# Order of SyncE's transfers in a fused top-k attention and MLP kernel: outputs and values ahead of the transposing transfers, queries and keys half a pair sooner

## The chip, the cores and the metric

The kernel runs on one core of one Trainium2 chip. A core has TensorE (PE; its weight loads are shown apart as PEld), VectorE (DVE), ScalarE (ACT), GpSimd (POOL) and SyncE (SP). SyncE computes nothing: it issues the transfers of this kernel, one after the other in program order, and sixteen DMA engines carry them out. The metric is the device time of one execution in microseconds (us).

## The reference

Two blocks follow each other. The first is attention over 8 batches of 8 heads, 576 positions and head size 64, in which every query keeps its 32 largest scores:

```python
scores = scale * np.matmul(q, k.transpose(0, 1, 3, 2))
kth = np.partition(scores, -top_k, axis=-1)[..., -top_k:-top_k + 1]
scores = np.where(scores >= kth, scores, -1000000000.0)
attn = np.exp(scores - max); attn = attn / (sum + 1e-09)
attn_out = np.matmul(attn, v)
```

The second takes the attention output as 4608 rows of 512 and sends them through a hidden layer of 2048: `h = x @ w_in`, `g = h * sigmoid(1.702 * h)`, `out = g @ w_out`. Everything is float32.

## The kernel before, in words

**Slots and pairs.** The work of the attention is cut into 144 slots, 18 for each batch `b`. A slot is 128 query rows of two heads: of one pair of heads `hp` (16 full slots of a batch, `t` = 0 to 3 and `hp` = 0 to 3), or the last 64 rows of two pairs of heads (two "ends" slots). An even batch has its full slots first and then its ends, an odd batch the other way round. From slot 25 on (`COLLECTED`), the function `joined_pair(n)` does one pair of slots `n`, `n + 1` per call, so `n` is odd, and what engines do within a pair is in the order in which this function calls things. Everything before is in an order written out by hand (`ORDER`), which the change does not touch.

**What happens to one slot.** TensorE computes the scores into PSUM, ScalarE copies them out (`sc`), VectorE finds the 32 largest by rounds of MAX8 and MATCH_REPLACE8 on `ranked`, ScalarE masks and takes exponentials (`pr`), GpSimd divides by the sum (`normalize`). Then the probabilities have to be transposed. `split` (line 613) lets ScalarE separate the 16-bit halves and writes them to DRAM (`rows`), and `turn_by_dma` (line 621) reads them back with a transposing transfer into `pt`. `pt` has two buffers, so a new transposing transfer can only be issued once TensorE has read the buffer of two slots before. From `pt` and the values `v_l`, `v_e`, TensorE computes the attention output.

**TensorE's run of scores.** Once per pair, `joined_section` (line 1426) runs on TensorE: first the attention outputs of slots `n - 5` and `n - 4` (matmuls into the tile `mixed`, reading `pt` and `v_l`), then the scores of two new slots (`s_ps`). It reads the values of slot `n - 5` first and, after 32 matmuls, those of slot `n - 4`. In the pairs that begin at the slots `18 b + 1` and `18 b + 3` these are the last slots that use the values of batch `b - 1`; the list `VALUES` (line 972) therefore makes `load_v` due there: heads in two halves at `18 b + 1` and `18 b + 3` for an even `b`, both halves at `18 b + 3` for an odd `b`.

**The MLP beside it.** `hidden` puts the first layer into the tile `unit`, `project` the second into the two banks `po`, in four units for each block of 128 rows, two units per pair; so a block is complete every second pair. Then `leave_parts` (line 921) lets ScalarE bring the banks to `raws`, GpSimd adds the parts up in two portions of three operations (`merge_some(3)`), and the last of them puts the output's two DMAs (`bring_out`, line 936) on a list `writes`. `write_all` (line 426) issues what is on that list. The next `leave_parts` writes the same part of `raws`, and so has to wait until these DMAs have read it.

**Queries and keys.** For each pair of heads, `load_both` (line 390) issues four DMAs into the one buffer `qk_l`; two or more slots later `prepare_by_dma` (line 394) lets ScalarE split them into `halves`, which frees the buffer; these are written to DRAM (`qk_rows`), and a transposing transfer brings them into `qk_t` later still. When these fall due stands in `READY` (line 969); `dues` (line 1207) collects what is due in the two slots of a pair, and `begin(0)` and `begin(1)` issue it in the middle and at the end of the pair.

**SyncE's order within a pair**, before: the transposing transfer of slot `n - 3` (`turn_due`); `rows` of slot `n - 1`; the transposing transfer of `n - 2`; `write_all` (outputs and `qk_rows`); `begin(0)` (values, queries and keys); `rows` of slot `n`; `write_all`; `begin(1)`.

Of the kernel before, what the change touches and what calls it, by code (L numbers as in the profile page):

```python
# [145 lines left out]
def kernel(  # L146
# [279 lines left out]
    def write_all():  # L426
        while writes:
            writes.pop(0)()
# [27 lines left out]
    PER = N // B  # L456
    st = [{} for _ in slots]

    def head_at(n, i):

        return 1 - i if n % 2 and slots[n][0] > 0 else i
# [76 lines left out]
    def exponentials(n, between=lambda: None):  # L538

        mask(n)  # L540
        between()
        exps(n)
# [78 lines left out]
    def turn_by_dma(n):  # L621

        rows = st[n]["rows"]
        pt = st[n]["pt"] = ptp.tile([P, 2 * NF + 1, P], F32, name="pt")
        nc.sync.dma_start_transpose(out=pt[:].bitcast(U16), in_=rows[:].rearrange("q h k -> (q h) k"))
# [330 lines left out]
    def leave_all():  # L956
        while leaving:
            leaving.pop(0)()
# [4 lines left out]
    def at(n, fn, *args):  # L963
        later.setdefault(n, []).append((fn, args))
# [4 lines left out]
    READY = (-15, -11, -7, -3), (-17, -13, -9, -5)  # L969
# [16 lines left out]
    for b in range(1, B):  # L986
        for hp in range(NP):
            if b > 1:
                earlier = 2 * ((b, hp) > (2, 1))
                at(b * PER + (READY[b % 2][hp] - 4 if earlier else (-19, -13)[hp]), load_both, b, hp)  # L990
                if (b, hp) != (2, 0):
                    at(b * PER + READY[b % 2][hp] - earlier, prepare_by_dma, b, hp)
            else:
                at(b * PER + FETCH_1[hp], load_both, b, hp)
        for hps, n in VALUES[b % 2 if b == 1 else b % 2 + 2].items():
            at(b * PER + n, load_v, b, *hps)
# [210 lines left out]
    def dues(n):  # L1207

        preparing = (prepare_by_dma,)
        todo = [later.pop(m, []) for m in (n, n + 1)]  # L1210
        assert not any(fn in preparing for fn, _ in todo[1])

        def begin(i):
            for fn, args in todo[i]:
                if fn not in preparing:
                    fn(*args)

        some = [(fn, args) for fn, args in todo[0] if fn in preparing]

        def prepare_some():  # L1220
            if some:
                fn, args = some.pop(0)
                fn(*args)

        return begin, prepare_some
# [3 lines left out]
    def find(m, at):  # L1229

        for i, op in enumerate(topk(m) if live(m) else [lambda: None] * 14):
            op()
            if i == 7 and live(m) and live(m + 1):
                pair_up(m + 1)
            if i == at and live(m - 1):
                invert(m - 1)
            if i > 1 and len(unfinished) > (2 if m == SETTLED + 1 else 0):
                finish_one()
# [187 lines left out]
    def joined_section(new, held):  # L1426

        begun = set()
        ends, rest = [], []
        for s, m in enumerate(held):  # L1430
            b, t, hps = slots[m]
            pt = st[m]["pt"]
            for p in range(2 if t == NF else 1):
                cols = slice(p * TAIL, (p + 1) * TAIL) if t == NF else slice(0, P)
                to = slice(s * P + cols.start, s * P + cols.stop)
                main, tail = vv[b, hps[p]]
                for i in range(2):
                    on, j = slice(i * TAIL, (i + 1) * TAIL), head_at(m, i)
                    ends.append((i, j, to, tail[on, j, :], pt[on, NF, cols]))
                for c in range(NF):  # L1440
                    for i in range(2):
                        rest.append((None, head_at(m, i), to, main[:, head_at(m, i), c, :], pt[:, MAIN[i] + c, cols]))
            st[m].clear()

        def score(n, i, p, first, count):
            b, t, hps = slots[n]
            cols = slice(t * P + p * TAIL, t * P + (p + 1) * TAIL) if t < NF else slice(FULL, S)
            on = slice(head_at(n, i) * D, (head_at(n, i) + 1) * D)
            keys = slice(FIRST[i] + first, FIRST[i] + first + count)
            return qT[b, hps[p]][on, cols], kT[b, hps[p]][on, keys]  # L1450

        def last_keys(r):
            of = [(n, head_at(n, r), p) for n in new for p in range(2)]
            at = lambda n, i: TAILS + n % 2 * P + i * TAIL
            return [(r, p, slice(at(n, i), at(n, i) + TAIL), *score(n, i, p, FULL, TAIL)) for n, i, p in of]

        def first_keys(n, r):
            i = head_at(n, r)
            for p in range(2):
                to = score_banks[n % 2][p * TAIL : (p + 1) * TAIL, i, :]  # L1460
                lhsT, rhs = score(n, i, p, 0, FULL)
                nc.tensor.matmul(to, lhsT=lhsT, rhs=rhs)

        upper = [x for x in ends if x[0] == 0] + last_keys(0)
        lower = last_keys(1) + [x for x in ends if x[0] == 1]
        halves = [x[1] for x in rest + upper + lower]
        count = iter(range(len(halves)))

        def mix(parts):
            for _, j, cols, lhsT, rhs in parts:  # L1470
                k = next(count)
                nc.tensor.matmul(
                    joined[0][j * D : (j + 1) * D, cols],
                    lhsT=lhsT,
                    rhs=rhs,
                    start=j not in halves[:k],
                    stop=j not in halves[k + 1 :],
                )

        def mark():  # L1480
            nc.tensor.drain(fusable=True).then_inc(parted, 1)
            parts_done.append(None)

        mix(rest)
        ahead = max(0, min(2, len(upper) - 2))
        mix(upper[:ahead])
        for n in new[:1]:
            first_keys(n, 1)
        mix(upper[ahead:-1])
        mark()  # L1490
        mix(upper[-1:])
        mark()
        for n in new[:1]:
            first_keys(n, 0)
        for n in new[1:]:
            first_keys(n, 1)
            first_keys(n, 0)
        nc.tensor.wait_ge(parted, len(parts_done))
        mix(lower)

    def copy_keys(n):
        sc = st[n]["sc"] = keys_ring[0].tile([P, 2, S], F32)
        nc.scalar.copy(out=sc[:, :, 0:FULL], in_=main_keys(n))

    def copy_last_keys(n):
        nc.scalar.copy(out=st[n]["sc"][:, :, FULL:S], in_=tails(n))

    def project_next():
        leave_all()
        project_one()  # L1510

    def turn_due(m):
        if live(m) and m > COLLECTED - 2:
            turn_by_dma(m)

    def joined_pair(n):

        begin, prepare_some = dues(n)
        held = [m for m in (n - 5, n - 4) if live(m) and m > COLLECTED - 4]
        new = [m for m in (n + 2, n + 3) if live(m)]  # L1520
        leave_all()
        if live(n - 1):
            exponentials(n - 1)
        if n == COLLECTED:
            combine()
        find(n, 10)
        joined_section(new, held)
        turn_due(n - 3)
        tanh(True)
        prepare_some()  # L1530
        for m in new[:1]:
            copy_keys(m)
        if held:
            x_of(held, joined[0][:, 0 : 2 * P].rearrange("p (s r) -> p s r", s=2))
        for m in new[:1]:
            copy_last_keys(m)
        project_next()
        leave_all()
        hidden(joined[1][:])
        if live(n - 1):  # L1540
            normalize(n - 1)
            split(n - 1)
        turn_due(n - 2)
        write_all()
        gate()
        begin(0)
        if live(n):
            bounds(n)
        combine()
        merge_some(3)  # L1550
        if live(n):
            mask(n)
            exps(n)
        tanh(True)
        for m in new[1:]:
            copy_keys(m)
            copy_last_keys(m)
        prepare_some()
        find(n + 1, 10)
        project_next()  # L1560
        if n == COLLECTED:
            project_next()
        hidden(joined[1][:])
        if live(n):
            normalize(n)
            split(n)
        write_all()
        while turns:
            turns.pop(0)()
        begin(1)  # L1570
        gate()
        if live(n + 1):
            bounds(n + 1)
        combine()
        merge_some(3)
# [76 lines left out]
```

## Time and profile before

| what | value |
|---|---|
| time, median of 3 runs (lowest to highest) | 1363.76 us (1361.4 to 1366.74) |
| the profiled execution's own time | 1358.13 us |
| its span in the profile | 1356.4 us |
| granted TensorE clock, mean over the span | 0.995 |
| busy, PE / DVE / ACT / POOL | 1330.3 / 1266.5 / 1163.8 / 978.8 us |
| share of the chain that ended last, PE / DVE / ACT / DMA / SyncE's queue | 84 / 6 / 3 / 3 / 2 % |
| transposing transfers `pt<-rows` | 136, median 6.1 us from issue to landing |
| values `v_l<-in_v_dram`, 512 KB each | 12, median 5.2 us from issue to landing |

Rows of the profile name an engine, a line, an operation and what it writes and reads (`mixed<-pt,v_l`); a line can be that of a helper (line 132 here), so the tiles tell the groups apart. SPq is SyncE's queue: what it shows as duration is the time for which SyncE is occupied with issuing a transfer, which lands later. In brackets stand the idle time of an engine before an instruction and what ended it. Such a releaser is inferred: where several semaphores are waited for, it can be a neighbour of the true one.

### The profile page before, as it was taken

The page shows a single profiled execution, that of the slowest core. Times are in us where ns is not written, and L with a number is a line of the kernel's source. Part 1 is how long each engine was busy: PE and PEld are TensorE (multiplying, and loading weights), DVE is VectorE, ACT ScalarE, POOL GpSimd, SP SyncE. Part 2 cuts the span into 40 slices and gives each one's busy share as a digit, 9 for nine tenths or more (in the row PEclk, how much of TensorE's full clock was granted, in tenths as well). Part 3 has the DMA queues.
Part 4 walks back from the last instruction along what each step waited for, and adds up shares of the span by engine and source line. Part 5 has one row for each costly group of instructions (what it writes and reads, how often), then busy time and mean ns, then how long its engine had stood idle before and what let it go on. Part 6 is the DMA issues. An engine that isn't in the chain of part 4 may idle for free.

```text
span 1356.4 us, 54099 instructions
## 1 busy us (share of the span) xinstructions
PE 1330.3 (98%) x22528; PEld 1207.0 (89%) x22528; DVE 1266.5 (93%) x3369; ACT 1163.8 (86%) x1872; POOL 978.8 (72%) x1788
## 2 busy tenths in 40 slices
PE   8999999999999999999999999999999999999998
PEld 6777579999999999899999999899999998999998
DVE  7999999999999999899999999999999999999902
ACT  6999998999989889899988988799999888888831
POOL 3889887777777777677777777777777777767761
PEclk8999999999999999999999999999999999999999
DMA  8445868898898787998999778988999887655640
GB/s 250 158 135 158 202 156 200 204 204 201 211 224 200 167 200 181 217 195 199 201 228 201 183 176 181 214 205 200 198 214 212 187 184 162 163 146 147 155 117 17
DMA packets 532325, 249.26 MB, mean 184 GB/s; under 512 B 463728, under 2 KB 510320, under 8 KB 532080
## 3 DMA queue, kind: packets, MB, share of 16 engines
q1 hardware_dynamic: 531648, 245.52, 78.3%
q8 instruction: 176, 2.88, 0.9%
q14 instruction: 69, 0.57, 0.1%
q10 hardware_dynamic: 432, 0.30, 0.1%
HBM read 46.01 MB, written 104.60 MB: 111 GB/s over the span
## 4 chain that ended last, share of the span: by engine, by line
PE 84%; DVE 6%; ACT 3%; DMA 3%; SPq 2%; issue 1%; POOL 1%; DVEq 0%; ACTq 0%; POOLq 0%
PE unit L132 30%; PE po L132 28%; PE mixed L132 11%; PE s_ps L132 7%; PE po L133 4%; DVE ranked L133 3%; DVE top L133 2%; PE ph L133 2%; SPq L132 2%; PE s_ps L133 2%; PE o L133 1%; DMA v_l<-in_v_dram 1%; ACT sc L133 1%; PE tp L133 1%; DVE ranked L132 1%
## 5 line engine op out<-in xcount | busy, mean ns | idle before, releaser
L132 DVE MAX8 top<-ranked 128x8 f32<-128x288 f32 (+1 forms) x952 | 519.4, 600 | 0.0
L132 PE MATMUL unit<-xT,win 128*64 128x128 f32 x7936 | 454.2, 273 | 0.0
L132 PEld LDWEIGHTS unit<-xT,win 128*64 128x64 f32 x7936 | 437.4, 137 | 0.0
L132 DVE MATCH_REPLACE8 ranked<-top,ranked 128x288 f32<-128x288 f32 x714 | 385.7, 547 | 0.0
L132 PE MATMUL po<-wout,th 128*64 128x128 f32 x4128 | 337.5, 274 | 0.0
L132 POOL TENSOR_TENSOR th<-th,th 128x128 f32<-128x128 f32 x374 | 273.8, 732 | 29.9
L132 POOL TENSOR_SCALAR pr<-pr,rden 128x576 f32<-128x576 f32 x240 | 176.6, 746 | 114.0 <-DVE rden L132 102.5
L132 PE MATMUL po<-raws,th 128*64 128x128 f32 x3096 | 256.6, 273 | 0.0
L132 PEld LDWEIGHTS po<-wout,th 128*64 128x64 f32 x4128 | 243.9, 137 | 9.9 <-issue 9.3
L132 ACT COPY sc<-pr 128x2304 uint16<-128x2304 uint16 x96 | 203.9, 2124 | 42.1 <-POOL pr L132 41.7
L132 PEld LDWEIGHTS po<-raws,th 128*64 128x64 f32 x3096 | 186.6, 137 | 0.0
L132 ACT ACTIVATE pr<-sc,low 128x576 f32<-128x576 f32 x192 | 146.4, 767 | 0.0
L132 PE MATMUL s_ps<-qk_t 64*64 64x512 f32 x936 | 140.8, 597 | 0.8 <-DMA qk_t<-qk_rows 0.7
L132 ACT ACTIVATE sc<-sc,cut 128x576 f32<-128x576 f32 x192 | 138.8, 776 | 1.4
L132 DVE TENSOR_TENSOR ranked<-s_ps,sc 128x576 f32<-128x576 f32 x188 | 133.1, 752 | 0.2 <-ACT sc L132 0.2
L132 PE MATMUL mixed<-pt,v_l 128*64 128x128 f32 (+1 forms) x2144 | 118.3, 264 | 5.7 <-DMA v_l<-in_v_dram 3.0
L132 POOL TENSOR_SCALAR some<-den 128x2 f32<-128x2 f32 x120 | 26.4, 220 | 129.6 <-ACT pr L132 124.6
L132 PEld LDWEIGHTS mixed<-pt,v_l 128*64 128x64 f32 x2144 | 110.2, 137 | 6.3 <-DMA qk_l<-in_q_dram 2.8
L132 POOL TENSOR_TENSOR th<-th 128x128 f32<-128x128 f32 x250 | 114.7, 459 | 0.4
L132 ACT ACTIVATE th<-unit 128x512 f32<-128x512 f32 x124 | 72.5, 585 | 48.3 <-PE unit L132 48.2
L133 DVE MAX8 top<-ranked 128x8 f32<-128x576 f32 (+1 forms) x200 | 111.8, 594 | 0.1
L132 ACT COPY sc<-s_ps 128x1024 f32<-128x1024 f32 x93 | 95.1, 1023 | 9.8 <-PE s_ps L132 9.6
(132 smaller groups left out, 2045.4 us busy)
## 6 DMA issues: line engine op xcount, KB each, us to landing
rows<-sc SPq DMA_DIRECT2D x112, 576.0 KB, 3.9
qk_rows<-halves SPq DMA_DIRECT2D x24, 576.0 KB, 4.8
rows<-spare SPq DMA_DIRECT2D x24, 576.0 KB, 4.0
out_dram<-raws SPq DMA_DIRECT2D x68, 128.0 KB, 3.2
raws<-in_moe_w_in_dram SPq DMA_DIRECT2D x16, 512.0 KB, 4.7
raws<-in_moe_w_out_dram SPq DMA_DIRECT2D x16, 512.0 KB, 4.0
qk_l<-in_q_dram SPq DMA_DIRECT2D x28, 256.0 KB, 4.5
qk_l<-in_k_dram SPq DMA_DIRECT2D x28, 256.0 KB, 4.3
```

The costliest lines, as they stand in the source:

```text
L132: return do(*args, **kwargs)
L133: self.engines.collected.append(lambda: do(*args, **kwargs))
```

## The change

SyncE's order is altered in three ways, all of them in the part from slot 25 on. Nothing is added to the computation and nothing is removed.

- Right after `joined_section`, and before the transposing transfer of slot `n - 3`, `write_all` is called once more. Outputs that the previous pair's second `merge_some` completed are issued there, and no longer in the middle of the pair. The two other calls of `write_all` remain.
- `load_v`, if it is due in `begin(0)`, is issued right behind that, also before the transposing transfer of `n - 3`. For this, `begin` takes a list of functions to which it restricts itself, and strikes off what it has issued.
- `load_both` falls due one slot earlier for all pairs of heads after `(2, 2)`: at `READY - 5` in place of `READY - 4`. Since that is an even slot, the four DMAs move from `begin(0)` of one pair to `begin(1)` of the pair before.

```diff
-                at(b * PER + (READY[b % 2][hp] - 4 if earlier else (-19, -13)[hp]), load_both, b, hp)
+                at(b * PER + (READY[b % 2][hp] - (5 if (b, hp) > (2, 2) else 4) if earlier else (-19, -13)[hp]), load_both, b, hp)
...
-        def begin(i):
-            for fn, args in todo[i]:
-                if fn not in preparing:
+        def begin(i, only=None):
+            for what in list(todo[i]):
+                fn, args = what
+                if fn not in preparing and (only is None or fn in only):
+                    todo[i].remove(what)
                     fn(*args)
...
         joined_section(new, held)
+        write_all()
+        begin(0, (load_v,))
         turn_due(n - 3)
         tanh(True)
         prepare_some()
```

## The prediction

> **What bounds the kernel now.** I read the page's first part, then the chain, then sums over windows cut at points of the chain, then SyncE's timeline.
>
> ```profile
> span 1356.4 us, 54099 instructions
> ## 1 busy us (share of the span) xinstructions
> PE 1330.3 (98%) x22528; PEld 1207.0 (89%) x22528; DVE 1266.5 (93%) x3369; ACT 1163.8 (86%) x1872; POOL 978.8 (72%) x1788
> ```
>
> TensorE is busy 98% of the span, VectorE 93%. The chain, from the pair that begins at slot 57 (a place where new values come in):
>
> ```profile
> 529.81 3.21 PE po L132 x56
> ...
> 539.37 6.03 DMA v_l<-in_v_dram
> 548.99 3.21 PE po L132 x56
> ```
>
> A "po x56" piece of 3.21 us opens the same unit in every pair, so the distance between two of them is a pair's time. Cutting there:
>
> ```profile
> 269.73:512.30 242.57, 242.57 (x4370) 226.00 (x4372) 240.67 (x643) 219.53 (x342) 177.24 (x342) 1.00 0.88 198
> 512.30:1253.32 741.02, 734.50 (x13346) 684.88 (x13348) 726.84 (x1934) 653.56 (x1025) 536.32 (x1031) 1.00 0.86 192
> 529.81:548.99 19.18, 17.73 (x354) 16.71 (x356) 19.18 (x52) 14.81 (x24) 15.94 (x30) 1.00 0.94 226
> 846.19:867.26 21.07, 17.95 (x354) 16.75 (x356) 21.07 (x58) 15.91 (x26) 17.59 (x32) 1.00 0.91 206
> 1111.15:1130.27 19.12, 18.39 (x314) 16.61 (x316) 19.12 (x52) 15.80 (x26) 12.75 (x24) 1.00 0.94 185
> 1165.10:1184.01 18.91, 17.76 (x355) 16.76 (x356) 18.91 (x53) 14.38 (x24) 15.67 (x29) 1.00 0.79 197
> ```
>
> Columns: window, its length, then busy time and instructions of PE, PEld, DVE, ACT, POOL, the granted clock, the DMA engines' share, GB/s. The first stretch is the pairs from slot 27 to slot 55, 14 of them: 242.57 / 14 = 17.326 us each, with PE busy throughout. That is the floor. The second stretch, slots 55 to 139, is 42 pairs, which would take 727.7; it takes 741.02. So 13.3 us lie above TensorE's floor, and this is the most that any order of transfers can give back. Three odd batch boundaries hold 1.85 + 3.74 + 1.58 = 7.2 of it (lengths less 17.33), the pair at 1111 holds 1.8, and 4.3 are in pieces under 1 us.
>
> Not all is a wait:
>
> ```profile
> 508.05:525.38 17.33, 17.33 (x316) 16.14 (x314) 17.33 (x48) 16.33 (x26) 12.58 (x25) 1.00 0.74 175
> 525.38:542.89 17.51, 17.51 (x356) 16.64 (x354) 17.51 (x48) 16.02 (x26) 13.26 (x26) 1.00 0.76 197
> ```
>
> A pair that reads ends slots has 40 matmuls more and takes 0.18 more without idling. Two such pairs at each of three boundaries make 1.1. This leaves 12.2 us of real waits: 6.6 at the boundaries, 1.8, and 3.8 in pieces. VectorE is full too in the first row (17.33 of 17.33), so it can't catch up what it once lost.
>
> What the waits are:
>
> ```profile
> ACT raws L132 <- DMA out_dram<-raws: 18.2, 17, 2.5
> ...
> ACT halves L132 <- DMA qk_l<-in_k_dram: 7.9, 5, 3.6
> ...
> PEld s_ps L132 <- DVE ranked L132: 6.8, 15, 0.9
> ```
>
> ```profile
> 542.89 1.10 PE L132 MATMUL mixed<-pt,v_l 128*64 128x64 f32 x32
> 545.45 1.15 PE L132 MATMUL mixed<-pt,v_l 128*64 128x64 f32 x32 [1.46 <-DMA v_l<-in_v_dram]
> ```
>
> ```profile
> 548.07 2.11 ACT L132 COPY halves<-qk_l 128x2304 uint16<-128x2304 uint16 x1 [2.91 <-DMA qk_l<-in_k_dram]
> ```
>
> ```profile
> 556.74 0.17 DVE L132 RECIPROCAL rden<-some 128x2 f32<-128x2 f32 x1 [1.70 <-POOL some L132]
> ```
>
> At a boundary TensorE waits for the second half of the values, then ScalarE 2.91 for the keys, and some 9 us on, VectorE idles 1.70 at the end of that chain. VectorE comes late from there on, and TensorE pays in small pieces, when it waits for VectorE to release a bank of scores (15 times). ScalarE's waits for the output's DMAs (17 times) feed the same. So I count the 3.8 as fed by the very transfers that the change moves.
>
> **The change, part by part.** SyncE around the first boundary:
>
> ```profile
> 523.98 0.96 SPq L132 DMA_DIRECT2D rows<-sc  x1
> 529.92 2.71 SPq L132 DMA_TRANSPOSE pt<-rows  x1
> 532.67 0.58 SPq L132 DMA_DIRECT2D rows<-sc  x1
> 533.37 3.94 SPq L132 DMA_TRANSPOSE pt<-rows  x1
> 537.36 0.58 SPq L132 DMA_DIRECT2D v_l<-in_v_dram  x1
> ...
> 541.32 2.24 SPq L132 DMA_DIRECT2D qk_l<-in_q_dram  x2
> 543.61 2.00 SPq L132 DMA_DIRECT2D qk_l<-in_k_dram  x2
> ```
>
> ```profile
> L132 SPq DMA_TRANSPOSE pt<-rows x120: 2227/3294/5071, 269.9 to 1304.6; - x120
> ...
> DMA to landing us min/median/max: 4.3/6.1/8.2
> ```
>
> *Queries and keys.* Four DMAs, 541.32 to 545.61, 4.3 us of SyncE. They move to the end of the pair before: behind the `rows` that end at 524.94, so until 529.24. SyncE idles there until 529.92, when TensorE's run has ended and the first transposing transfer may go. Cost 0; the idle stretch hides it, with 0.7 to spare. Without that cover the transposing transfers would be up to 4.3 late. The second, issued at 533.37 and landing 6.1 later at 539.5, is needed when the second 32 matmuls can begin, 542.89 + 1.10 = 543.99: 4.5 of slack, so 0 at the median even then. The buffer is free: `halves` of the previous pair of heads was copied early in the same pair. Gain: ScalarE's 7.9 us of waiting.
>
> *Outputs.* Their adds on GpSimd end at 508.84 + 1.15 = 509.99, and the transposing transfer behind them goes at 512.43:
>
> ```profile
> 508.84 1.15 POOL L132 TENSOR_TENSOR raws<-raws 128x128 f32<-128x128 f32 x2
> ```
>
> ```profile
> 512.43 3.30 SPq L132 DMA_TRANSPOSE pt<-rows  x1
> ```
>
> Two DMAs occupy SyncE 1.3 (below), so they fit into 509.99 to 511.3. Cost 0, hidden by SyncE's wait for TensorE. They go some 10 us earlier, and the 18.2 us for which ScalarE waits on them fall away. In the pair at 1111 they also clear the way for the transfer that TensorE then lacks:
>
> ```profile
> 1119.88 1.29 SPq L132 DMA_DIRECT2D out_dram<-raws  x2
> 1121.21 3.29 SPq L132 DMA_TRANSPOSE qk_t<-qk_rows  x1
> ```
>
> `qk_t` goes 1.3 earlier; together with a ScalarE that is less late I take the whole 1.8, and 1.3 as the lower bound.
>
> *Values, even batches.* One half per pair, (541.32 - 537.36) / 2 = 2.0 us ahead of two transposing transfers with 4.5 of slack: 0. The values themselves are not waited for there now (the first stretch holds such a boundary and loses nothing).
>
> *Values, odd batches.* Both halves, 4.0 us, go from 529.92 to 533.9. Then the first transposing transfer, median 3.29, to 537.2 (landing at 533.9 + 6.1 = 540.0, needed at 542.89). Then `rows`, long ready, 0.6, to 537.9. Then the second transposing transfer: landing at 537.9 + 6.1 = 544.0 against a need of 543.99. The values were issued by 533.9 and took 6.03 in the chain, so they land by 540. The wait for values goes; what is late next is the transposing transfer, by nothing at the median. Bounds for it: with both transfers at their shortest it lands 2.9 early, with both at their longest (5.07 and 8.2) 3.9 late. I take 0.3 for each boundary, near the median, since a wait can't be negative; 0.9 in all, and 0 to 11.7 for the range.
>
> The Trainium skill's "DMA: Bandwidth & Descriptors", section "Issuing engines are not separate DMA queues", says that the time to initiate a DMA is usually small beside the DMA, and that all queues share the 16 engines and interleave. By that, order on SyncE would buy little and this term would be nothing. The row differs: a transposing transfer holds SyncE for 2.2 to 5.1 us of the 4.3 to 8.2 until it lands, so I go by the row.
>
> *Sum:* 6.6 + 1.8 + 3.8 - 0.9 = 11.3 us. The profiled execution's own time is 1358.13 (span 1356.4 and 1.7 around it), so it would become 1346.8. The median of the runs shown lies 5.6 above this execution, for a reason that one profile can't give; off the median, 1363.76 - 11.3 = 1352.
>
> **The rivals.**
>
> *The wait only changes its name.* If bytes and not SyncE set the pace, the two transposing transfers, `rows` and both halves of the values still finish together at 545.4, only that `pt` is now last. The boundaries give nothing and 5.6 (1.8 + 3.8) remain: 1358. For it: a DMA share of 0.94 and 0.91 in two of the three windows. Against it: 0.76 in the pair at 525.38, with SyncE idle from 524.94 to 529.92, and queries and keys no longer in the way. This is what the page's shared engines would mean; a share of 0.79 in the third window, which waited all the same, speaks against.
>
> *VectorE takes the gain back.* It is full at 17.33 per pair, so if its own work is a little above the floor, waits removed on TensorE come back as waits for banks of scores: no change, 1361 to 1366. Against it: 14 pairs in a row at 17.326, with VectorE idle for 242.57 - 240.67 = 1.9 us.
>
> *Slower: SyncE stands at the output.* If GpSimd's adds ended late, the output's DMA would hold both transposing transfers of that pair, where before it stood behind them. It decides from adds that end 2.4 - 1.3 = 1.1 us later than in the row at 508.84, plus the 4.5 of slack: 5.6 us. This occurs in every second pair, 28 times in the 56; at 0.6 us beyond that point it costs 17 us: 1380. Against it: GpSimd is 72% busy, and these adds run 2.4 us ahead of need.
>
> **How the numbers follow.** Waits gone as summed: 0.74, with a range of its own from 1345 (all 12.2, and the 5.6 between profile and median also such waits: 1346, less a little) to 1356. Changed name: 0.12, 1358. VectorE: 0.07. SyncE stands: 0.07, 1380. The range 1345 to 1361 takes in the first two with the larger boundary waits. About 0.5%, 6.8 us, is what a measurement tells from no change: below 1356.9 is faster. That is the first case and a third of the second, 0.78; within it 0.15; slower 0.07.
>
> **What would show it.** Right: the distance of the "po x56" pieces is 17.33 almost everywhere and 17.51 at six pairs; no wait of `mixed` for `v_l`; no wait of `halves` for `qk_l` nor of `raws` for `out_dram`; TensorE's waits for `ranked` near nothing; between slots 55 and 139, 729 to 731 us in place of 741.02. Wrong: waits of `mixed` for `pt` at the three boundaries of 1 us or more, SyncE waiting for GpSimd's `raws`, or the small pieces still there with no ScalarE wait in front of them.

## The result and the profile after

| kernel | median (lowest to highest), us | before on the same chip, us | ratio, 95% interval |
|---|---|---|---|
| the change | 1354.28 (1349.36 to 1356.01), 6 runs | 1363.57 (1361.4 to 1366.74), 6 runs | 0.9923 [0.9899, 0.9946] |

The change makes the kernel 0.77% faster. The median is 1354.28 us where the forecast was 1352, and the profiled execution took 1349.36 us where the sum said 1346.8. The first part of the page and its chain, of the changed kernel:

```profile
span 1347.6 us, 54130 instructions
...
PE 1326.2 (98%) x22528; PEld 1203.9 (89%) x22528; DVE 1265.6 (94%) x3369; ACT 1164.1 (86%) x1872; POOL 978.8 (73%) x1788
...
PE 77%; DVE 12%; ACT 4%; POOL 2%; DMA 2%; issue 2%; SPq 0%; DVEq 0%; ACTq 0%; POOLq 0%
```

SyncE's queue held 2% of the chain before and holds 0% now. The share of DVE rose from 6 to 12%: from 269 to 387 us, ahead of a short wait of TensorE for `pt`, the chain now passes over VectorE, while TensorE is busy there for 119.20 of 119.41 us. So this share is no loss. The windows show more. They are cut at the same pieces ("po x56") as those of before: the pairs of slots 27 to 55; those of 55 to 139; the first two odd boundaries; and the pair that was at 1111. The columns are those of the prediction.

```profile
268.59:511.59 243.00, 242.79 (x4371) 226.02 (x4372) 239.83 (x642) 218.64 (x342) 176.74 (x341) 1.00 0.91 198
...
511.59:1244.57 732.98, 730.48 (x13346) 682.09 (x13348) 728.12 (x1936) 655.90 (x1025) 537.96 (x1033) 1.00 0.86 194
...
529.10:546.95 17.85, 17.73 (x355) 16.75 (x356) 17.85 (x48) 15.92 (x25) 14.69 (x29) 1.00 1.14 237
841.78:861.30 19.52, 17.73 (x354) 16.75 (x356) 19.52 (x54) 16.50 (x25) 16.28 (x31) 1.00 1.09 230
...
1103.94:1122.92 18.98, 18.39 (x314) 16.61 (x316) 18.98 (x51) 15.76 (x26) 12.99 (x25) 1.00 0.92 186
```

The 42 pairs from slot 55 became 741.02 - 732.98 = 8.0 us shorter. The 14 pairs ahead of them became 243.00 - 242.57 = 0.4 longer. The profiled executions differ by 8.8; the missing 1.1 lies before slot 27, which the change does not touch, and in the profiles of all kernels shown here the joined pairs began anywhere between 262.9 and 266.9 us, so that 1.1 is chance. Above the floor of 42 x 17.326 = 727.7 there are now 5.3 us where there were 13.3. The first boundary costs 0.52 in place of 1.85 (each length less 17.33), the second 2.19 in place of 3.74, and the pair "at 1111" 1.65 in place of 1.8. What TensorE and ScalarE still wait for:

```profile
ACT pr L132 <- DMA qk_rows<-halves: 9.8, 8, 2.3
...
PE mixed L132 <- DMA pt<-rows: 2.0, 2, 1.8
...
PEld s_ps L132 <- DMA qk_t<-qk_rows: 1.5, 1, 1.5
```

`mixed` waits no more for `v_l`, `raws` no more for `out_dram`. In their place stand a wait for the transposing transfer and the old one for `qk_t`. ScalarE has a new wait of 9.8 us, before `pr`, for the DMA that reads `halves`. Among the waits of the odd-only order below the same wait is listed with 6.6 us in 7 times, while TensorE waits for no DMA there from slot 27 on, so there it costs the end nothing.

SyncE at the first boundary, to be laid beside the same place in the prediction:

```profile
524.19 1.70 SPq L132 DMA_DIRECT2D qk_l<-in_q_dram  x2
525.94 1.40 SPq L132 DMA_DIRECT2D qk_l<-in_k_dram  x2
527.43 0.54 SPq L132 DMA_DIRECT2D v_l<-in_v_dram  x1
528.08 1.73 SPq L132 DMA_DIRECT2D v_e<-in_v_dram  x2
529.86 0.60 SPq L132 DMA_DIRECT2D v_l<-in_v_dram  x1
530.51 1.29 SPq L132 DMA_DIRECT2D v_e<-in_v_dram  x2
531.84 3.99 SPq L132 DMA_TRANSPOSE pt<-rows  x1
535.93 0.51 SPq L132 DMA_DIRECT2D rows<-sc  x1
536.50 3.36 SPq L132 DMA_TRANSPOSE pt<-rows  x1
```

Queries, keys and both halves of the values now stand in one block ahead of the transposing transfers, which start 2.6 and 3.8 us later than before, counted from the pair's "po x56" piece (529.10 here, 529.81 before).

### The profile page after: what moved, and what is told of

Read it like the earlier page. It is cut to its first block, busy times and chain, and to the rows that moved or that the text cites. A ratio compares the mean times of both kernels' runs of the same rounds, so it can differ in the third digit from the quotient of the medians.

```text
span 1347.6 us, 54130 instructions
## 1 busy us (share of the span) xinstructions
PE 1326.2 (98%) x22528; PEld 1203.9 (89%) x22528; DVE 1265.6 (94%) x3369; ACT 1164.1 (86%) x1872; POOL 978.8 (73%) x1788
## 4 chain that ended last, share of the span: by engine, by line
PE 77%; DVE 12%; ACT 4%; POOL 2%; DMA 2%; issue 2%; SPq 0%; DVEq 0%; ACTq 0%; POOLq 0%
PE unit L132 27%; PE po L132 26%; PE mixed L132 10%; PE s_ps L132 6%; DVE ranked L132 3%; DVE top L132 3%; DVE ranked L133 3%; PE po L133 3%; DVE top L133 2%; DMA pt<-rows 2%; PE ph L133 2%; PE s_ps L133 1%; PE o L133 1%; ACT sc L133 1%; POOL th L132 1%
```

## The experiments

Each difference is against the changed kernel unless it says otherwise. Three groups ran on one chip each, every group beside runs of the kernel before; a ratio is against those.

**One part of the change alone.** Queries and keys alone: the kernel before, with only the line on `load_both` altered.

```diff
-                at(b * PER + (READY[b % 2][hp] - 4 if earlier else (-19, -13)[hp]), load_both, b, hp)
+                at(b * PER + (READY[b % 2][hp] - (5 if (b, hp) > (2, 2) else 4) if earlier else (-19, -13)[hp]), load_both, b, hp)
```

> Only queries and keys go half a pair sooner. Theory: ScalarE's 7.9 us of waiting for keys become nothing, VectorE keeps its pace behind the boundaries, so most pieces under 1 us go: 2 to 4 us faster; the waits for v_l stay, 1 to 1.5 us each (the one of 3.1 at slot 95 becomes about 1.5, as the pair no longer begins late). Rival (the pieces come from elsewhere): 741 us for the stretch less at most 1.

Outputs alone:

```diff
-                at(... READY[b % 2][hp] - (5 if (b, hp) > (2, 2) else 4) ..., load_both, b, hp)
+                at(... READY[b % 2][hp] - 4 ..., load_both, b, hp)
...
         write_all()
-        begin(0, (load_v,))
```

> Only the outputs go ahead of the transposing transfers; values, queries and keys stay where they were. Theory (waits of TensorE at the boundaries come from values and from queries and keys, the small pieces from ScalarE's waits): ScalarE's 18 us of waiting for the outputs fall to nothing; the values are waited for at the three odd boundaries as before (1 to 3 us each); the transfer of qk_t at the pair near 1111 goes 1.3 us earlier. The stretch from slot 55 to slot 139, 741.0 us before, becomes 737 to 739: 2 to 4 us faster. Rival (VectorE is the bound, its own work takes back what ScalarE gains): 741 as before, no gain.

Values alone:

```diff
-                at(... READY[b % 2][hp] - (5 if (b, hp) > (2, 2) else 4) ..., load_both, b, hp)
+                at(... READY[b % 2][hp] - 4 ..., load_both, b, hp)
...
-        write_all()
         begin(0, (load_v,))
```

> Only the new values go ahead; outputs, queries and keys stay. Theory: no wait of TensorE for v_l at the boundaries, in its place a wait for pt under 1 us, 4 to 6 us faster; but ScalarE still waits near 3 us for keys at each odd boundary, VectorE idles some us behind it, and pieces under 1 us remain. Rival (the wait only changes its name, bytes set the pace): the boundaries keep their 7.2 us above the floor with pt as what is waited for, gain under 1 us.

| alone | median, us | before | ratio, 95% interval |
|---|---|---|---|
| queries and keys | 1355.71 | 1360.37 | 0.9957 [0.9941, 0.9974] |
| outputs | 1357.53 | 1360.37 | 0.9976 [0.9958, 0.9993] |
| values | 1358.69 | 1360.37 | 0.9988 [0.9976, 1.0001] |

The three add up to 0.79%, about what the whole change gives. The values, by which the prediction explained the largest term, are the smallest, and their interval reaches 1. The waits with queries and keys alone:

```profile
ACT raws L132 <- DMA out_dram<-raws: 15.6, 18, 1.5
...
PE mixed L132 <- DMA v_l<-in_v_dram: 4.7, 3, 2.3
...
PEld s_ps L132 <- DVE ranked L132: 1.3, 3, 0.7
```

With the values alone:

```profile
ACT raws L132 <- DMA out_dram<-raws: 27.4, 22, 3.5
...
PEld s_ps L132 <- DVE ranked L132: 8.2, 14, 1.2
...
ACT halves L132 <- DMA qk_l<-in_k_dram: 5.7, 3, 2.9
```

And with the outputs alone:

```profile
ACT halves L132 <- DMA qk_l<-in_k_dram: 9.7, 6, 4.6
...
PEld s_ps L132 <- DVE ranked L132: 1.5, 3, 0.8
```

There were two suspects for the pieces under 1 us, and neither makes them alone. With the keys early, TensorE's waits for `ranked` fall from 6.8 us (15 times) to 1.3 (3 times) although ScalarE still waits 15.6 us for the outputs. With the outputs early they fall to 1.5 (3 times) although ScalarE still waits 9.7 us for the keys. Where both are late they stay (8.2, 14 times).

In the profiles the stretch of 42 pairs takes 739.84 us (queries and keys), 739.85 (outputs) and 739.86 (values), each only 1.2 us less than before; the first two hold some us at half the clock, as is shown further down. Each of the three missed what was expected of the profile or of the time: the outputs' stretch lies between the two values expected, the values gained 1.7 us in the median and not 4 to 6, with waits for `pt` of up to 2.0 us, and with early queries and keys the stretch became 1.2 us shorter where 2 to 4 were expected, though the median fell by 4.7.

**The change without one part.** Without early queries and keys:

```diff
-                at(... READY[b % 2][hp] - (5 if (b, hp) > (2, 2) else 4) ..., load_both, b, hp)
+                at(... READY[b % 2][hp] - 4 ..., load_both, b, hp)
```

> The changed kernel without its third part: queries and keys stay in the middle of the pair. Theory (keys that come late at an odd boundary hold ScalarE near 3 us, and VectorE, which has no slack, pays it back in pieces): ScalarE waits 4 us or more for qk_l, pieces under 1 us return, the stretch from slot 55 to slot 139 at 736 to 739, 3 to 5 us slower than the changed kernel. Rival (pieces came from the outputs): 733 to 735.

Without early outputs:

```diff
         joined_section(new, held)
-        write_all()
         begin(0, (load_v,))
```

> The changed kernel without its first part: outputs stay in the middle of the pair, values, queries and keys go early. Theory (outputs feed ScalarE's waits and, in the pair before slot 125, stand ahead of qk_t): ScalarE waits 15 us or more for the outputs again, the wait for qk_t at slot 125 is 1 us longer than in the changed kernel, the stretch from slot 55 to slot 139 at 734 to 736, 1 to 3 us slower than the changed kernel. Rival (ScalarE's waits cost nothing once queries and keys come early, as the run with these alone suggests): less than 1 us slower.

Without early values:

```diff
         write_all()
-        begin(0, (load_v,))
```

> The changed kernel without its second part: values stay in the middle of the pair. Theory: TensorE waits for v_l at the three odd boundaries, 1.2 to 4 us each as in the run with queries and keys alone, and no longer for pt; the stretch from slot 55 to slot 139 at 735 to 738, 2 to 4 us slower than the changed kernel. Rival (the wait only changes its name): the same time, 733 to 735.

| left out | median, us | before | ratio, 95% interval |
|---|---|---|---|
| queries and keys | 1356.99 | 1361.29 | 0.9966 [0.995, 0.9982] |
| outputs | 1357.57 | 1361.29 | 0.9968 [0.9947, 0.9988] |
| values | 1350.57 | 1361.29 | 0.9933 [0.9913, 0.9954] |

Without early values the time is that of the changed kernel. Its waits and its stretch of 42 pairs:

```profile
PE mixed L132 <- DMA v_l<-in_v_dram: 4.3, 3, 2.3
```

```profile
509.71:1246.26 736.55, 732.12 (x13348) 682.84 (x13347) 727.79 (x1935) 652.19 (x1024) 537.07 (x1032) 1.00 0.86 193
```

Once outputs and queries are out of the way, the values behind the transposing transfers cost 4.3 us of waiting, and ahead of them they cost 2.0 for `pt` instead. In the stretch this leaves 736.55 - 732.98 = 3.6 us for the values (1.9 against the second profile of the changed kernel, below), which the medians don't resolve. It lies at the odd boundaries: without early values these lose 6.5 us in all, as before the change, and with them 2.4. Some 1.7 of the 6.5 is a stretch at half the clock (below).

Without early outputs TensorE waits longer at the second boundary than in the kernel before. SyncE there:

```profile
837.88 1.33 SPq L132 DMA_DIRECT2D out_dram<-raws  x2
839.26 1.58 SPq L132 DMA_DIRECT2D qk_rows<-halves  x2
840.98 0.98 SPq L132 DMA_DIRECT2D rows<-sc  x1
842.01 2.56 SPq L132 DMA_DIRECT2D qk_l<-in_q_dram  x2
844.61 2.36 SPq L132 DMA_DIRECT2D qk_l<-in_k_dram  x2
847.07 0.55 SPq L132 DMA_DIRECT2D v_l<-in_v_dram  x1
...
851.05 5.28 SPq L132 DMA_TRANSPOSE pt<-rows  x1
856.43 0.53 SPq L132 DMA_DIRECT2D rows<-spare  x1
857.02 3.55 SPq L132 DMA_TRANSPOSE pt<-rows  x1
```

```profile
864.25 1.98 PE L132 MATMUL mixed<-pt,v_l 128*64 128x64 f32 x32 [3.21 <-DMA pt<-rows]
```

From 837.88 to 860.57 SyncE has no gap over 0.2 us. With the outputs back in the middle of the pair, all behind them goes later, and the second transposing transfer lands 3.21 us late. The stretch takes 742.30 us, longer than before the change and outside the expected 734 to 736; of this some 3 us are the clock at this wait (below), for the 32 matmuls take 1.98 us here and took 1.15 behind such a wait before. The idle time that the prediction let cover queries and keys is partly there because the outputs have left that place. Without early queries and keys the stretch takes 738.99, as the theory had it, but not by the way it named: TensorE's waits for `ranked` are 2.6 us (7 times), and the larger losses are waits for `pt`, at two odd boundaries and at the slots 39 and 111, and the one for `qk_t`.

**Number of DMAs or bytes.** The changed kernel fetches both halves of an odd batch's values with six DMAs. One kernel does it with three:

```diff
-    VALUES = {}, {(0, 1, 2, 3): 2}, {(0, 1): 1, (2, 3): 3}, {(0, 1): 3, (2, 3): 3}
+    VALUES = {}, {(0, 1, 2, 3): 2}, {(0, 1): 1, (2, 3): 3}, {(0, 1, 2, 3): 3}
```

> As the changed kernel, but at odd batches the values of all four pairs of heads come in three transfers (1024 KB and twice 128 KB) in place of six: the same bytes, some 1.9 us less of SyncE's time ahead of the two transposing transfers. Theory (SyncE's issuing sets when pt lands): the wait of 1.79 us for pt at slot 95 and the 0.12 at slot 59 go, 1.5 to 2 us faster than the changed kernel, the stretch at 731. Rival (the bytes set it): pt lands as late as with six, 733 as the changed kernel.

The other with twelve (each 512 KB transfer of `v_l` as four of 128 KB, in odd batches after the first):

```diff
-        nc.sync.dma_start(
-            v_main[:, pairs, :, :, :].rearrange("p h j t d -> p (h j) (t d)"),
-            v[b, heads, 0:FULL, :].rearrange("j (p t) d -> p j (t d)", t=NF),
-        )
+        heads_of_each = range(heads.start, heads.stop) if b > 1 and b % 2 else (None,)
+        for h in heads_of_each:
+            some = heads if h is None else slice(h, h + 1)
+            at_h = slice(None) if h is None else slice(h - heads.start, h - heads.start + 1)
+            nc.sync.dma_start(
+                v_main[:, pairs, :, :, :].rearrange("p h j t d -> p (h j) (t d)")[:, at_h, :],
+                v[b, some, 0:FULL, :].rearrange("j (p t) d -> p j (t d)", t=NF),
+            )
```

> As the changed kernel, but at odd batches each half's 512 KB of values come as four transfers of 128 KB in place of one: the same bytes, six more transfers per boundary, some 3.6 us more of SyncE's time ahead of the transposing transfers. Theory (SyncE's issuing sets when pt lands): TensorE waits for pt at each of the three odd boundaries, 2 to 4 us longer than in the changed kernel, 8 us slower than it in all. Rival (bytes set it): pt lands as before, within 1 us of the changed kernel.

The changed kernel was run again beside the latter:

> The changed kernel once more, beside the three that follow, to see how far two of its executions differ. All theories: the stretch from slot 55 to slot 139 within 1.5 us of 733.0, waits of TensorE for pt at slot 95 and for qk_t at slot 125 again, 7 to 11 us faster than before.

| DMAs per odd boundary | median, us | before | ratio, 95% interval |
|---|---|---|---|
| 3 | 1348.56 | 1360.37 | 0.9922 [0.9904, 0.9939] |
| 6 (the change again) | 1350.8 | 1359.42 | 0.9938 [0.9919, 0.9957] |
| 12 | 1359.78 | 1359.42 | 0.9996 [0.9982, 1.001] |

With the same bytes, six more DMAs at three boundaries cost 9.0 us and take back the whole gain of the change. The kernel with twelve, SyncE at the first boundary and TensorE's wait behind it, then its stretch and its waits:

```profile
532.31 3.04 SPq L132 DMA_DIRECT2D v_l<-in_v_dram  x4
...
536.79 3.12 SPq L132 DMA_DIRECT2D v_l<-in_v_dram  x4
...
541.31 3.11 SPq L132 DMA_TRANSPOSE pt<-rows  x1
...
545.09 4.07 SPq L132 DMA_TRANSPOSE pt<-rows  x1
```

```profile
552.07 1.91 PE L132 MATMUL mixed<-pt,v_l 128*64 128x64 f32 x32 [2.61 <-DMA pt<-rows]
```

```profile
517.76:1257.40 739.64, 733.63 (x13347) 683.54 (x13348) 727.62 (x1934) 653.42 (x1024) 536.75 (x1032) 1.00 0.84 192
```

```profile
PE mixed L132 <- DMA pt<-rows: 8.1, 4, 2.7
```

The values' two 512 KB transfers hold SyncE for 6.16 us (3.04 + 3.12) where they held it for 1.14 (0.54 + 0.60), and the DMA engines are no busier (0.84 against 0.86 in the stretch). The added time is SyncE's, and TensorE waits for the transfers queued behind. Three of these four waits lie at the odd boundaries. The fourth, 2.07 us at 391.4, lies at an even batch, which the edit does not touch; why it came there is open. Not all of the 9.0 is waiting. Behind three of the four waits TensorE runs for 3.41 us at half its clock; the first row is this kernel, the second the changed one at the same place behind its longest wait:

```profile
552.20:555.50 3.30, 3.30 (x54) 2.75 (x57) 3.30 (x12) 0.00 (x0) 3.06 (x7) 0.50 1.18 235
...
857.88:861.18 3.30, 3.30 (x80) 2.48 (x79) 3.30 (x10) 1.49 (x2) 3.22 (x5) 1.00 1.06 201
```

So each of these three waits cost about 1.7 us on top of its length, by estimate (half of 3.41); their pairs lost 3.9, 4.4 and 4.6 us with waits of 2.1, 2.6 and 2.7. The runs agree: the two of this kernel with the highest mean clock, 0.996, took 1355.26 and 1355.81 us, the two with the lowest, 0.991, took 1360.16 and 1362.37. By estimate from these runs the DMAs as such cost about 5 of the 9.0 us, and this clock most of the rest.

The Trainium skill's "DMA: Bandwidth & Descriptors", section "Issuing engines are not separate DMA queues", says that issue time is usually small beside the transfer. It does not fit here, as the prediction held: the 5.0 us more at the first boundary (4.1 and 3.9 at the others) are SyncE's issue time alone, and TensorE waits for them. Fewer DMAs than six gain at most a little: the intervals of the first two rows overlap.

**Towards a better order.** The first of these adds to the single load an earlier place for `qk_t`: its transposing transfers for the third and fourth pair of heads of odd batches fall due one slot sooner.

```diff
-    TURN = {2: -4, 3: -3}
+    TURN = {2: -5, 3: -4}
...
-    VALUES = {}, {(0, 1, 2, 3): 2}, {(0, 1): 1, (2, 3): 3}, {(0, 1): 3, (2, 3): 3}
+    VALUES = {}, {(0, 1, 2, 3): 2}, {(0, 1): 1, (2, 3): 3}, {(0, 1, 2, 3): 3}
```

> As the kernel with one load of values at odd batches, and with the transposing transfers of qk_t for the last two pairs of heads of odd batches due one slot earlier (TURN -5 and -4 in place of -4 and -3). Theory (each remaining wait is a transfer that SyncE issues too late): the wait at slot 125, 1.4 to 1.7 us, goes; the stretch from slot 55 to slot 139 at 729 to 731 us; 1.3 us faster than with one load alone. Rival (what is moved pushes another transfer late): a wait for pt of as much in the pair before it, the stretch at 731.7 as with one load alone.

The second keeps that and takes the early values back at even batches, where nothing had waited for them before. It was run in two of the groups.

```diff
-        begin(0, (load_v,))
+        if n // PER % 2:
+            begin(0, (load_v,))
```

> As the one before, but new values go ahead of the transposing transfers at odd batches only; at even batches, where half of them are due in each of two pairs and nobody waits for them, they stay in the middle of the pair. Theory (early values push the transposing transfers of even boundaries late): no wait of TensorE for pt at the slots 41, 77 and 113, the stretch from slot 27 to slot 55 at 242.6, 0.5 to 1.5 us faster than the one before. Rival (those waits are chance): no difference.

> The kernel with one load of values at odd batches, qk_t one slot earlier and even batches' values left in place, once more, to see whether its boundaries without a wait were chance: with early values at even batches too, the slots 59 and 95 waited 2.5 and 1.6 us for pt, though the order of SyncE around them is the same. Theory (the order leaves the transposing transfers room): no more than 1 us in all above 42 pairs at 17.326 and the six heavier ones, 728.8 to 729.9, 13 to 16 us faster than before. Rival (how long a transposing transfer behind 1280 KB of values takes is chance): 1 to 5 us at the slots 59, 95 or 131.

| kernel | median, us | before | ratio, 95% interval |
|---|---|---|---|
| single load, `qk_t` sooner | 1349.89 | 1359.42 | 0.9917 [0.99, 0.9933] |
| the same, even batches as before | 1345.53 | 1359.42 | 0.989 [0.9872, 0.9908] |
| the same again | 1346.55 | 1361.29 | 0.9902 [0.9883, 0.992] |

With the earlier `qk_t` the wait at slot 125 is gone, but the stretch takes 733.76 us, above the 729 to 731 expected, because `pt` is waited for at two boundaries. The odd-only order is faster than the kernel before and the changed kernel. Its windows for the slots 27 to 55 and 55 to 139, and SyncE in the pair that lacked `qk_t`:

```profile
269.83:512.40 242.57, 242.57 (x4370) 226.00 (x4372) 240.64 (x643) 220.81 (x343) 177.54 (x342) 1.00 0.88 199
...
512.40:1241.23 728.83, 728.83 (x13347) 680.99 (x13348) 726.18 (x1934) 654.34 (x1024) 536.40 (x1030) 1.00 0.88 195
```

```profile
1097.28 3.48 SPq L132 DMA_TRANSPOSE qk_t<-qk_rows  x1
1100.80 1.41 SPq L132 DMA_DIRECT2D out_dram<-raws  x2
```

TensorE is busy for 728.83 of 728.83 us. That is 727.7 and the 1.1 for the 40 matmuls more in six pairs: the prediction's floor, reached, so no order of transfers gives more in this stretch. VectorE follows with 726.18. The second profile of this order takes 729.37 there, with 0.55 us lost at slot 77.

Seven profiles show what goes with the loss at an odd boundary. The table gives, for the first, second and third of them, the time from the pair's "po x56" piece to the issue of the second transposing transfer, and what TensorE lost in the pair behind (its length less 17.33 and less the 0.18 of such a pair):

| kernel | issued after, us | lost, us |
|---|---|---|
| the change | 7.4, 8.3, 6.7 | 0.3, 2.0, 0 |
| the change again | 7.7, 8.3, 7.3 | 0.8, 1.6, 0 |
| twelve DMAs | 9.8, 10.1, 8.7 | 4.4, 4.6, 0.9 |
| three DMAs | 7.5, 6.9, 5.7 | 0.3, 0, 0 |
| single load, `qk_t` sooner | 8.5, 7.2, 6.2 | 2.5, 1.7, 0 |
| the same, even batches as before | 6.6, 6.9, 6.9 | 0, 0, 0 |
| the same again | 7.1, 6.3, 6.6 | 0, 0, 0 |

Issued by 7.1 us it costs nothing; from 7.2 to 7.7 it costs 0 to 1.7; from 8.3 on 0.9 to 4.6, where the two largest, with twelve DMAs, hold 1.7 each of half clock. So the loss follows the moment at which SyncE comes to this transfer, and the change stands just at the edge.

Why the last two orders differ at the first two boundaries is not settled. The edit between them concerns other batches; yet in the profile without it the first transposing transfer held SyncE for 5.98 and 5.22 us, with it for 4.21 and 5.45, and the values began up to 2.2 us sooner, counted in the same way. The second profile of the odd-only order loses nothing at the three boundaries either, with 5.22, 4.36 and 4.60 us for the first transfer. The medians differ by 4.4 us, but the intervals of the ratios still touch, and one profile against two can't say how much of this is the edit's.

**The clock behind long waits.** No expectation had this. In six of the fourteen profiles, and there within the joined pairs, the granted TensorE clock falls to 0.50 for 3.41 us, or twice that, at a long wait of TensorE: without early values and without early queries and keys, with queries and keys alone (once each, 3.41), with outputs alone and without early outputs (once each, 6.83), with twelve DMAs (three times, 3.41). In the first five it stands at the second odd boundary. These stretches begin between 1.0 us before and 1.4 us after the end of a wait of 1.97 us or more. Length alone does not decide: waits of 2.69 us (the kernel before), 2.26 and 2.18 passed without one. No shorter wait between the slots 27 and 139 had one, and neither had the change or the odd-only order in either profile. A profile of one part alone or of one part left out therefore measures this as well as the part, and the medians above may do so too, since the mean clock of the single runs of one kernel differs (with twelve DMAs, 0.991 to 0.996).

## Why the prediction was right, and which terms were not

- **TensorE's floor of 17.326 per pair, 1.1 that is no wait, 12.2 us of real waits.** Right, and the odd-only order shows it: with all waits gone the stretch takes 728.83.
- **6.6 us at the boundaries, less 0.9 for new waits: the second was mis-sized.** The waits for `v_l` and for the keys went, but the new ones for `pt` cost 0.34 + 2.01 + 0 = 2.4 (the two windows less 17.33 and less the 0.18 of each such pair; nothing at the third). At the second boundary the chain has this row:

```profile
850.12 7.50 DMA pt<-rows
```

  Its landing at 857.62 (850.12 + 7.50) is what TensorE waits for. The prediction took the medians, 3.29 for SyncE's time and 6.1 to landing; right behind the values the first of the two transfers held SyncE for 3.99 and 3.95 us at the first two boundaries (4.28 and 4.93 in the second profile), `rows` and the gaps beside it took 1.65 at the second boundary in place of 0.7, and the second transfer took 7.5 to land. The start was better than assumed: `v_l` begins at 527.43, before TensorE's run has ended, since it needs only the first part of the run over.
- **1.8 at `qk_t`: the term that failed.** 1.65 remain. The prediction let the two outputs hide in SyncE's wait for TensorE. It read that from the pair at 508.84; in this pair there is too little of the wait, because the previous `qk_t` stands in it:

```profile
1099.46 3.25 SPq L132 DMA_TRANSPOSE qk_t<-qk_rows  x1
1102.82 2.53 SPq L132 DMA_DIRECT2D out_dram<-raws  x2
1105.46 3.10 SPq L132 DMA_TRANSPOSE pt<-rows  x1
...
1113.45 3.50 SPq L132 DMA_TRANSPOSE qk_t<-qk_rows  x1
```

  Counted from the pair's "po x56" piece (1103.94, and 1111.15 before), the first `pt` goes at 1.5 where it went at 0.1, and the `qk_t` that TensorE lacks at 9.5 where it went at 10.1. So 0.6 was gained and not 1.3, and the outputs take 2.53 here in place of 1.3. With the earlier `qk_t` moved out of the way (the `TURN` edit) the wait is gone. It is also gone with the outputs alone: there the previous `qk_t` leaves SyncE 2.1 us ahead of the piece and not 1.2, the outputs take 1.3, and the `qk_t` that was lacking goes at 6.9. So the step can hold. Beside the other parts it failed (with outputs and one other part the pair still lost 1.2 and 2.0 us); why the outputs hold SyncE longer in the changed kernel (2.53, and 3.08 in its second profile) is open.
- **3.8 in pieces: right in size, and in cause as far as the runs reach.** Under 0.2 us of such pieces are left (1.1 in the second profile). The prediction fed them from ScalarE's waits for the keys and for the outputs. The kernels with one of the two early show that it takes both: moving either ends most of TensorE's waits for `ranked`.
- **"Cost 0" for values at even batches.** Off by 0.4: the stretch from slot 27 to 55, which holds such a boundary, takes 243.00. The odd-only order takes 242.57, as before the change. The second profile of the change takes 242.57 there too, but loses 0.4 at slot 111, the last even boundary. With values early and queries late the slots 39 and 111 lose 1.8 and 1.9, so in that profile the cost is not small.
- **"Cost 0" for queries and keys, hidden by SyncE's idle time.** True in the whole change. Alone it was not tested against that idle time, but the kernel without early outputs shows that the cover is made by the other part.

The sum for the profiled execution was 1346.8; it took 1349.4. That difference of 2.6 is 1.5 more at the boundaries, 1.65 at `qk_t`, 0.2 in pieces and 0.4 at an even batch, less 1.1 before slot 27. The 1.1 is luck: of the 11.3 us forecast, the pairs from slot 55 on gave 8.0 in the first profile and 6.4 in the second. Of the signs named beforehand, the waits for `v_l` and `out_dram` went and those for `qk_l` all but went (0.2 us), but the stretch took 732.98 us (734.63 in the second profile) and not 729 to 731, and one boundary of the three showed a wait for `pt` above 1 us, which stood among the signs of being wrong.

Of the rivals, "the wait only changes its name" is partly true: at two boundaries `pt` is now last. But not because bytes set the pace: with equal bytes, twelve DMAs make the second transposing transfer go 1.4 to 2.4 us later than six, and the kernel slower. "VectorE takes the gain back" is false: VectorE did its work in 728.83 us as well. "SyncE stands at the output" is false: SyncE's waits for GpSimd's `raws` are listed with 10.1 us in 2 times, as against 10.0 in 2 before the change. The median lies 4.9 above the profiled execution. The six runs spread over 6.7 us, and the profiled one had the highest mean clock (0.997); the three at 0.994 took 1353.9 to 1356.0, the two at 0.995 took 1350.1 and 1355.95. So part of the spread may be the clock; no profile of a slower run shows it.

## What to carry to other kernels

Where one engine issues all transfers, add up its issue time per iteration as for a compute engine: a DMA that can go early belongs ahead of long ones, but each that goes ahead delays the next, and here its count weighed more than its bytes. Read "hidden by the issuer's idle time" at every place where the moved step occurs, since another transfer can have taken that idle time in some of them. Cutting windows at a piece that recurs in each iteration gives the floor of the bound engine, and so the most that any such change can win. When a variant loses more than its waits are long, look at the granted clock in a window behind each wait.

## What was not expected of the hardware

How long a transposing transfer holds SyncE depends on what went out just before it. Its median was 3.29 us before the change. As the first one at the three odd boundaries it took 4.12 to 5.98 behind three DMAs of values (three kernels), 2.65 to 3.99 behind six (4.93 at most in the second profile), and 2.50 to 3.11 behind twelve, whose issue is the slowest. That fewer bytes are then still under way is an argument, and no run shows it. Splitting a 512 KB load into four made SyncE's part 3.04 us where it was 0.54, some 0.8 for each DMA of a quarter of the bytes. And a wait of TensorE of about 2 us or more went in eight cases with 3.41 or 6.83 us at half its clock, and in three cases without.
